# Seven block products instead of eight in six groups of layer one's second mixing product

## The chip, the core and the metric

The kernel runs on one core of a Trainium2 chip. The core has a matrix engine, TensorE (PE in the profile; PEld is its weight load), a vector engine, VectorE (DVE), a scalar engine, ScalarE (ACT), GpSimd (POOL), and SyncE (SP), from whose queue nearly all transfers are issued. The metric is device time in microseconds (us), the median over several executions.

## The reference

Two layers run over x of 2048 tokens by 1024 features in bf16. Each is an attention part and a mixing part, both with the residual added:

```python
x = x + _A_ref(_layernorm(x), A_wqkv, A_wo)
x = x + _B_ref(_layernorm(x), B_w1, B_b1, B_w2, B_b2)
# _A_ref: qkv = x @ wqkv; 32 heads of 32; each token looks at 8 tokens, 2 apart, up to itself;
#         softmax; the values, times wo
# _B_ref: h = _layernorm(x); u = gelu(h^T @ w1 + b1)     # over tokens: w1 is 2048 x 3584
#         y = u @ w2 + b2                                # w2 is 3584 x 2048; y, transposed, is added to x
```

Both layers use the same weights. The mixing part works along the tokens: its first product turns 2048 tokens into 3584 hidden units for each of 1024 features, the second turns them back.

## The kernel before

Tokens are kept in 16 tiles of 128: eight groups i, each with the even (c = 0) and the odd tokens (c = 1) of 256 neighbours. The hidden units are kept in 14 tiles `g[fb]` of 2 x 128 units by 1024 features.

**The first mixing product** (`gemm1`, L666) walks 14 blocks of 256 hidden units. Block 0 is a plain product. Blocks 1 to 13 are each computed as a 2 x 2 block product with seven block products of eight matmuls (L719) instead of eight, after sums and differences of blocks on both sides (the Strassen scheme, in the variant of Winograd). The sums need fp16 operands in a bounded range, so ACT scales the weights of each block by a power of two, which DVE derives from a bound: the largest absolute value of the block, from two reductions over the tiles (`top`), a trip through DRAM to all partitions (`share`) and a few small operations (`power`). In layer one the weight sums are computed and stored in DRAM (`keep_sums`); layer two loads them. In layer two it also scales the finished hidden tiles (`scale_g`, on DVE) and POOL forms differences of them (`hidden_sums`).

**The second mixing product of layer one** is plain (`gemm2`, L1013). For each group i, SP fetches its 256 columns of `w2` in four parts of 448 KB (`load_w2`). For each parity c, PE runs two chains of 28 matmuls of 128x128 by 512 (L1021), with every second column of the weights as its stationary operand. DVE adds the bias and the residual tile xs (L1023) and takes the statistics for the next layer's norm (L203, L205); ACT computes the root (L197, L198); DVE normalises (L211); SP stores the tile and transposes it into hT, layer two's input (L1028). Meanwhile DVE searches the `w2` tiles for their largest values (L1011, four parts per group), with which layer two scales `w2`: at the start of layer two all eight groups' bounds are shared in one trip (`share_w2`, L652) and turned into powers (`power_w2`, L659).

**The second mixing product of layer two** (`gemm2s`) already computes every group with seven block products of 14 matmuls (L908), in pairs of groups. Its moves and scalings are on ACT (L880), the weight sums on DVE. The order of the seven in one group: the first goes to a bank pa; a scaled copy of it is moved to a bank pb, where another accumulates on it; that sum is moved to a bank pc; and so on, so that the seven results are combined inside the accumulation banks, with a few moves by ACT between.

**What sets the order.** PE's instructions are issued in the order of `in_order` calls, those of another engine in the order of `chain_` calls, where each instruction is issued after the one before it on its engine. SP has one queue, in order. An entry that waits, such as a transpose waiting for its normalised tile, holds back everything behind it.

**Places.** Weight tiles turn over in a pool of nine (`wp`), residual tiles and temporaries in one of six (`x2`), values and small unit tiles in one of 16 (`vh`), the hidden tiles in one of 14 (`gop`), scaled weight pairs in one of two (`qp`), broadcasts in another of two (`pcp`). `Pm`, `kT` and `qB` belong to the attention and are free during the mixing part.

## Time and profile before

The time is 1223.34 us, the median of three runs (1223.07 to 1223.37). The profiled execution took 1223.0 us, and its span, from the first instruction to the last, is 1221.3 us. TensorE's granted clock is 1.00 throughout.

| stage, us of the span | length | PE busy | DVE | ACT | POOL | DMA share |
|---|---|---|---|---|---|---|
| start and value projection, layer one, 0 to 65 | 65.0 | 63.4 | 38.8 | 30.0 | 2.4 | 0.83 |
| attention, layer one, 65 to 203 | 138.0 | 134.9 | 110.2 | 95.1 | 0.0 | 0.28 |
| output projection, 203 to 262 | 59.0 | 58.6 | 50.1 | 27.4 | 23.6 | 0.59 |
| first mixing product, plain block, 262 to 274 | 12.0 | 11.9 | 9.4 | 10.4 | 12.0 | 0.64 |
| first mixing product, 13 blocks, 274 to 431.4 | 157.4 | 156.7 | 106.1 | 107.0 | 0.9 | 0.60 |
| second mixing product, 431.4 to 624.8 | 193.4 | 192.5 | 114.3 | 9.5 | 0.0 | 0.49 |
| value projection, layer two, 624.8 to 680 | 55.2 | 54.9 | 9.3 | 18.4 | 0.0 | 0.07 |
| attention, layer two, 680 to 820 | 140.0 | 136.8 | 96.0 | 95.7 | 0.0 | 0.20 |
| output projection and plain block, 820 to 891 | 71.0 | 70.5 | 52.9 | 34.3 | 35.8 | 0.65 |
| first mixing product, 13 blocks, 891 to 1048 | 157.0 | 156.3 | 31.2 | 64.8 | 28.1 | 0.53 |
| second mixing product, 1048 to 1221 | 173.0 | 169.2 | 111.3 | 58.6 | 5.8 | 0.37 |

The DMA share is the mean busy share of the core's 16 DMA engines. In the lines of the profile that follow, L12 is line 12 of the kernel; `out<-in` are tiles by the program's names; a group's line ends in its busy time, the mean of one instruction in ns, and the idle time ahead of its instructions with what ended it. A line of the timeline has start, length, engine, line, operation, tiles, shape and count; brackets give a wait and its releaser. A line of a stretch (A:B) has its length and then busy time and count of PE, PEld, DVE, ACT and POOL, the granted clock, the DMA share and GB/s. A line of the DMA list has the tiles, queue, kind, count, KB of each, and the median time from issue to landing.

### The profile page before, as it was taken

The page shows a single profiled execution, that of the slowest core. Times are in us where ns is not written, and L with a number is a line of the kernel's source. Part 1 is how long each engine was busy: PE and PEld are TensorE (multiplying, and loading weights), DVE is VectorE, ACT ScalarE, POOL GpSimd, SP SyncE. Part 2 cuts the span into 40 slices and gives each one's busy share as a digit, 9 for nine tenths or more (in the row PEclk, how much of TensorE's full clock was granted, in tenths as well). Part 3 has the DMA queues.
Part 4 walks back from the last instruction along what each step waited for, and adds up shares of the span by engine and source line. Part 5 has one row for each costly group of instructions (what it writes and reads, how often), then busy time and mean ns, then how long its engine had stood idle before and what let it go on. Part 6 is the DMA issues. An engine that isn't in the chain of part 4 may idle for free.

```text
span 1221.3 us, 20012 instructions
## 1 busy us (share of the span) xinstructions
PE 1205.6 (99%) x7946; PEld 559.8 (46%) x8088; DVE 729.6 (60%) x1298; ACT 551.2 (45%) x924; POOL 108.7 (9%) x107
## 2 busy tenths in 40 slices
PE   9999999999999999999999999999999999999998
PEld 4444444444444444444444444444444444444444
DVE  7558887888777346565650467778711212785664
ACT  5457775467666610000013577764543444432342
POOL 0000000290000000000000000002722112200000
PEclk9999999999999999999999999999999999999999
DMA  8922233566565635545520110234946564264520
GB/s 235 153 62 72 82 105 104 165 199 200 167 201 163 203 89 147 135 133 148 162 78 1 44 46 20 77 110 139 309 130 197 155 190 135 72 189 129 154 80 35
DMA packets 217837, 159.28 MB, mean 130 GB/s; under 512 B 46864, under 2 KB 193936, under 8 KB 214416
## 3 DMA queue, kind: packets, MB, share of 16 engines
q1 hardware_dynamic: 217744, 158.01, 44.7%
q8 instruction: 63, 1.03, 0.4%
q14 instruction: 30, 0.25, 0.1%
HBM read 115.49 MB, written 30.43 MB: 119 GB/s over the span
## 4 chain that ended last, share of the span: by engine, by line
PE 98%; issue 1%; DVE 0%; DMA 0%; ACT 0%; DVEq 0%
PE m L399 18%; PE s L719 12%; PE m L515 9%; PE s L1021 8%; PE m L719 8%; PE s L908 7%; PE a L719 6%; PE m L384 5%; PE m L1021 4%; PE a L1021 4%; PE m L908 4%; PE s L288 3%; PE a L908 3%; PE s L595 2%; PE s L430 2%; PE a L288 1%
## 5 line engine op out<-in xcount | busy, mean ns | idle before, releaser
L399 PE MATMUL m<-hT,wqk 128*128 128x512 bf16 x963 | 223.5, 379 | 6.3 <-issue 4.6
L446 DVE TENSOR_TENSOR Pm<-pc,band 32x640 bf16<-32x640 bf16 x256 | 123.6, 483 | 53.9 <-ACT pc L434 47.1
L399 PEld LDWEIGHTS <-wqk 128*128 128x128 bf16 x1024 | 95.3, 98 | 117.9 <-issue 10.7
L1021 PEld LDWEIGHTS <-w 128*128 128x128 bf16 x896 | 87.7, 98 | 105.7
L719 PEld LDWEIGHTS <-Sw 128*128 128x128 f16 x832 | 81.4, 98 | 98.1
L197 ACT ACTIVATE ln<-mv,eps 128x1 f32<-128x1 f32 x64 | 18.9, 295 | 230.4 <-DVE mv L205 185.1
L515 PE MATMUL m<-wo,oT 128*128 128x512 bf16 x500 | 110.8, 379 | 0.9 <-issue 0.3
L1021 PE MATMUL s<-g,w 128*128 128x512 bf16 x439 | 97.5, 379 | 0.5
L719 PEld LDWEIGHTS <-w 128*128 128x128 f16 (+1 forms) x624 | 61.1, 98 | 73.6
L609 POOL TENSOR_TENSOR T<-h 128x512 f16<-128x512 bf16 x16 | 18.4, 1152 | 809.9 <-DMA xr<-xb 560.9
L410 DVE COPY qB<-qs 32x512 bf16<-32x512 bf16 x136 | 38.2, 281 | 72.1 <-ACT qs L406 70.0
L515 PEld LDWEIGHTS <-oT 128*128 128x128 bf16 x512 | 49.6, 98 | 60.6 <-issue 1.9
L719 PE MATMUL s<-T,Sw 128*128 128x512 f16 x288 | 66.1, 379 | 0.0
L434 ACT ACTIVATE pc<-s,shift 128x320 bf16<-128x320 f32 x128 | 60.8, 531 | 11.2 <-PE s L430 11.2
L609 DVE TENSOR_TENSOR py<-pz,m 128x512 f32<-128x512 f32 x14 | 9.6, 688 | 92.5 <-PE m L719 66.2
L1011 DVE TENSOR_REDUCE mx<-w 128x1 f32<-128x1792 bf16 x32 | 63.0, 2010 | 0.0
L406 ACT CAST qs<-m 128x512 bf16<-128x512 f32 x64 | 37.5, 585 | 44.3 <-PE m L399 41.9
L403 ACT CAST kT<-m 128x512 bf16<-128x512 f32 x64 | 37.5, 585 | 41.9 <-PE m L399 38.8
L384 PE MATMUL m<-wv,hT 128*128 128x512 bf16 x251 | 55.2, 379 | 0.3
L522 DVE TENSOR_TENSOR xn<-m,xr 128x512 bf16<-128x512 f32 x64 | 44.1, 689 | 15.2 <-PE m L515 14.6
L719 PE MATMUL m<-T,Sw 128*128 128x512 f16 x224 | 52.9, 379 | 0.0
L719 PE MATMUL a<-h,w 128*128 128x512 bf16 x224 | 52.9, 379 | 0.0
(172 smaller groups left out, 1817.0 us busy)
## 6 DMA issues: line engine op xcount, KB each, us to landing
w<-in_B_w_dram SPq DMA_DIRECT2D x86, 512.0 KB, 5.6
w<-in_B_w_dram SPq DMA_DIRECT2D x32, 448.0 KB, 3.7
sd<-Sw SPq DMA_DIRECT2D x13, 1024.0 KB, 6.3
Sw<-sd SPq DMA_DIRECT2D x13, 1024.0 KB, 4.9
wqk<-in_A_wqkv_dram SPq DMA_DIRECT2D x16, 512.0 KB, 5.0
xa<-xn SPq DMA_DIRECT2D x32, 256.0 KB, 2.2
xs<-xa SPq DMA_DIRECT2D x32, 256.0 KB, 3.0
wo<-in_A_wo_dram SPq DMA_DIRECT2D x8, 512.0 KB, 5.4
```

What stands on the lines that cost most here:

```text
L288: r = nc.tensor.matmul(pss_[k][n][:], lhsT=hT[:, kt, cols(*order[k])], rhs=wv[kt // 2][:, kt % 2, n * 512:(n + 1) * 512], start=(kt == 0), ...
L384: nc.tensor.matmul(ps[:], lhsT=hT[:, kt, cols(c, i)], rhs=wv[kt // 2][:, kt % 2, n * 512:(n + 1) * 512], start=(kt == 0), stop=(kt == KD - 1))
L399: mm = nc.tensor.matmul(ps[:], lhsT=wts[part][:, kt, (g % 2) * P:(g % 2 + 1) * P], rhs=hT[:, kt, lo:lo + 512], start=(kt == 0), stop=(kt = ...
L410: nc.vector.tensor_copy(out=qB[u % 2][hp, h, ls], in_=qs[hp, :])
L434: nc.scalar.activation(out=pc[:, 2 * n:2 * n + 2].rearrange("p t h k -> p (t h k)"), in_=ss[n][:, 0:2 * HG * GW], func=ACT.Exp, scale=scal ...
L446: mm = nc.vector.tensor_tensor(out=Pm[rp, :, s0:s0 + HB, r * KG:r * KG + GW].rearrange("p h t k -> p t h k"), in0=pc[rp], in1=mk, op=ALU.mult)
L515: mm = nc.tensor.matmul(ps[:], lhsT=oT[g][:, cols(c, i)], rhs=wo[n][g // 4][:, g % 4, :], start=(g == 0), stop=(g == NG - 1))
L522: return nc.vector.tensor_tensor(out=xn[:, xs_], in0=pss_["o", n][:], in1=xr[:, xs_], op=ALU.add)
L719: r = nc.tensor.matmul(out, lhsT=lhs[:, k, :], rhs=rhs[k], start=start and k == 0, stop=stop and k == NI - 1, skip_group_check=True)
L908: r = nc.tensor.matmul(out, lhsT=lhs[k], rhs=rhs[k][:, cols_], start=start and k == 0, stop=k == K - 1, skip_group_check=True)
L1011: return nc.vector.tensor_reduce(out=mx2[:, i, n:n + 1], in_=w2t[n][:], op=ALU.max, axis=AX.XY, apply_absolute_value=True)
L1021: nc.tensor.matmul(ap, lhsT=w2t[ft // HF][:, ft % HF, c::DIL], rhs=g[ft // GF][:, ft % GF, lo:lo + w], start=(ft == 0), stop=(ft == FT - 1))
```

## The change

In layer one's second mixing product, groups 0 and 1 stay plain, in four chains of 28 matmuls each. Groups 2 to 7 are computed as 2 x 2 block products, with seven block products of 14 matmuls in place of eight. The blocks are: units of even and odd tiles on one side, the two halves of the features (`lo`, `hi`) and the two parities on the others. That needs the scaled hidden tiles (`scale_g`), which layer one did not have; differences of hidden tiles (T1 to T4: `NT3` on POOL during group 0; T2 on DVE at its end, T1 in group 1, T4 in groups 1 and 2); and for each group the powers of two of its weights before its sums are formed.

The bounds of these groups' weights therefore have to be known earlier. Each `w2` group is fetched once more in seven pieces of 256 KB, into spare places (`room`: `Pm`, then parts of hT not yet written), from the third block of the first mixing product on; ACT takes a bound of a piece with one pass of absolute values and a sum over each partition (`bound_act`); a few are taken by DVE (`bound_dve`). `share_w2` and `power_w2` now work on two groups at a time and stand at places written out by hand: for groups 2 and 3, 4 and 5, 6 and 7 in this stage, for 0 and 1 in layer two's first mixing product, after 28 reductions in layer two's attention (`top_load`, `top2`).

Within a group i from 2 on, ACT also scales the four quarters of the weights of group j = i + 1 (`scaled`: A22 = q[j][:, 0], S1 = q[j][:, 1], U2, U4, four instructions each), DVE forms their sums (`mix`), and `corner` and `quarter` bring the results back to scale with bias and residual. The order of every queue in the stage, SP's included, is now written out. The 32 searches on DVE, `gemm2` and the one `share_w2` at layer two's start go.

```diff
...
+    def share_w2(i0, nb=NB2):
+        i1 = i0 + 2
+        chain_("DVE", lambda: nc.vector.tensor_reduce(out=mx3[:, i0:i1], in_=mx2[:, i0:i1, 0:nb], op=ALU.max, axis=AX.X))
+        bcw[i0] = pcp.tile([P, P, 2], FP32, name="bcw", tag="pc")
+        nc.sync.dma_start(out=mxw[i0 // 2][:], in_=mx3[:, i0:i1])
+        return nc.sync.dma_start(out=bcw[i0][:], in_=mxw[i0 // 2][:].partition_broadcast(P))
+
+    bcw = {}
+
...
+        chain_("DVE", powers, i0, i1, bcw.pop(i0)[:].rearrange("p q i -> p i q"), cs2, ci2)
...
+        chain_("DVE", ts, inv2[:, i0:i1], ci2[:, i0:i1], gi[:])
+        chain_("DVE", ts, ncs2[:, i0:i1], cs2[:, i0:i1], -1.0)
+        chain_("DVE", ts, k[:], cs2[:, i0:i1], gs[:])
...
+        chain_("DVE", tt, nc.vector, bia[:, i0:i1, 1], bia[:, i0:i1, 1], k[:], ALU.mult)
...
+    room = [Pf[:, n * 1024:(n + 1) * 1024].rearrange("p (f s) -> p f s", s=256) for n in range(NPM)]
...
+    def fetch(dst):
+        i, n = jobs.pop(0)
+        fetched.append((i, n, dst))
+        return nc.sync.dma_start(out=dst,
+                                 in_=w2_v[:, 4 * n:4 * n + 4, i * 256:(i + 1) * 256])
...
+    def bound_act(i, n, src):
+        return nc.scalar.activation(out=src, in_=src, func=ACT.Abs, accum_out=mx2[:, i, n:n + 1])
...
+    def bounds(eng, n):
+        for _ in range(n):
+            i, k, src = fetched.pop(0)
+            chain_(eng, bound_act if eng == "ACT" else bound_dve, i, k, src)
...
+        def late_work(fb):
+            n = fb - (NFB - 3)
+            for f in range(*((0, 4), (4, 9), (9, 13))[n]):
+                chain_(V, scale_g, f)
...
+            if first and fb > 1:
+                for _ in range(2 if fb < 5 else 1):
+                    with tc.issue_after(kept.ins):
+                        fetch(room.pop(0))
+            if first and fb >= 4:
+                bounds(A, 1)
...
+            if first and fb == NFB - 3:
+                hidden_scale()
...
+            if first and fb >= NFB - 3:
+                late_work(fb)
...
+            if not first and fb == 2:
+                share_w2(0, 2 * NB2)
+            if not first and fb == 5:
+                power_w2(0)
         if first:
-            chain_(V, hidden_scale)
...
+    def gemm2f(g, src, dst, seam):
...
+        def scaled(i, out, f, c, ns=range(4)):
+            for n in ns:
+                chain_(A, lambda: nc.scalar.activation(out=part(out, n), in_=raw(i, f, c, n), func=ACT.Identity,
+                                                       scale=cs2[:, i:i + 1]))
...
+        def mix(out, x, y, op):
+            for o, a_, b_ in zip(pieces(out), pieces(x), pieces(y)):
+                chain_(V, tt, nc.vector, o, a_, b_, op)
...
+        def load_x(i):
+            for c in range(DIL):
+                xs[i, c] = x2("xs")
+                chain_("SP", nc.sync.dma_start, out=xs[i, c][:], in_=rows(src, c, i))
...
+        def load_w(i):
...
+                chain_("SP", nc.sync.dma_start, out=w[i][n][:], in_=w2_v[:, f0:f1, i * 256:(i + 1) * 256])
...
+        def corner(i, c, h, src_):
+            tq = x2("tq", [P, 512], FP32)
+            chain_(A, move, tq[:], src_, scale=gi[:], bias=b2_sb[:, i, c:c + 1])
...
+        def corner_add(i, c, h):
+            x = xs[i, c][:, halves[h]]
+            chain_(V, tt, nc.vector, x, tqs.pop((i, c, h))[:], x, ALU.add)
+            stat_half(i, c, h)
...
+        def quarter(i, c, h, src_):
+            x = xs[i, c][:, halves[h]]
+            chain_(V, lambda: nc.vector.scalar_tensor_tensor(out=x, in0=src_, scalar=inv2[:, i:i + 1], in1=x, op0=ALU.mult,
+                                                             op1=ALU.add))
...
+        def aggregate(i, c):
+            chain_("SP", nc.sync.dma_start, out=rows(dst, c, i), in_=xs[i, c][:])
+            mvs[i, c] = st("mv", [P, 2])
+            chain_(V, lambda: nc.vector.bn_aggr(out=mvs[i, c][:], in_=t[i, c][:]))
+
+        def root(i, c):
+            ln, rss[i, c] = st("ln", [P, 1]), st("rs", [P, 1])
+            chain_(A, lambda: nc.scalar.activation(out=ln[:], in_=mvs[i, c][:, 1:2], func=ACT.Ln, bias=eps1[:], scale=1.0))
+            chain_(A, lambda: nc.scalar.activation(out=rss[i, c][:], in_=ln[:], func=ACT.Exp, scale=-0.5))
...
+        def normalise(i, c):
+            xn = kT[1]
+            chain_(V, norm_dve, xn[:], xs[i, c][:], mvs[i, c][:, 0:1], rss[i, c][:])
+            chain_("SP", nc.sync.dma_start_transpose, out=hT[:, :, cols(c, i)], in_=xn[:])
+
+        def refill(n):
+            for _ in range(n):
+                chain_("SP", fetch, room.pop(0))
...
+        load_w(0)
+        load_x(0)
+        room[:] = [hT[:, m:m + 4, (c * NI + i) * P:(c * NI + i + 2) * P] for i in (6, 4) for c in range(DIL) for m in (0, 4)]
+        refill(8)
+        load_w(1)
+        chain_(A, ln_exp_table)
+        grp = [(0, 1), (1, 1), (0, 0), (1, 0)]
...
             for ft in range(FT):
-                nc.tensor.matmul(ap, lhsT=w2t[ft // HF][:, ft % HF, c::DIL], rhs=g[ft // GF][:, ft % GF, lo:lo + w],
-                                 start=(ft == 0), stop=(ft == FT - 1))
-            nc.vector.scalar_tensor_tensor(out=xo[:, lo:lo + w], in0=ap, scalar=b2_sb[:, i, c:c + 1],
-                                           in1=xs[:, lo:lo + w], op0=ALU.add, op1=ALU.add)
-        nc.sync.dma_start(out=dst, in_=xo[:])
-        mean, rs = stats(xo, 1.0, eps1)
-        last["DVE"] = norm_dve(xs[:], xo[:], mean, rs[:])
-        nc.sync.dma_start_transpose(out=hT[:, :, cols(c, i)], in_=xs[:])
-        for n in range(2 * c, 2 * c + 2):
...
+        bk = [[t_[:] for t_ in two("s") + two("s")], [t_[:] for t_ in two("a") + two("m")]]
+        in_order(tokens, 0, 0)
+        bounds(A, 4)
+        corner(0, 0, 1, bk[0][0])
+        corner_add(0, 0, 1)
+        share(2)
+        in_order(tokens, 0, 1)
+        bounds(A, 4)
+        for k in range(K):
+            chain_(G, tt, nc.gpsimd, T3(k), B22[k], B12[k], ALU.subtract)
+        corner(0, 1, 1, bk[0][1])
+        corner_add(0, 1, 1)
...
+        in_order(tokens, 0, 2)
+        bounds(A, 3)
+        del room[:5]
+        corner(0, 0, 0, bk[0][2])
+        corner_add(0, 0, 0)
...
+        root(0, 0)
+        normalise(0, 0)
+        in_order(tokens, 0, 3)
+        load_w(2)
+        load_x(1)
+        bounds(A, 1)
+        refill(5)
+        units_a(2)
+        units_b(2)
+        units_c(2)
+        corner(0, 1, 0, bk[0][3])
+        corner_add(0, 1, 0)
+        aggregate(0, 1)
+        scaled(2, q[2][:, 0], 1, 1)
+        root(0, 1)
+        t2(*range(4))
+        normalise(0, 1)
+        t2(*range(4, K))
+        in_order(tokens, 1, 0)
+        corner(1, 0, 1, bk[1][0])
+        scaled(2, q[2][:, 1], 0, 1)
+        scaled(2, U2[2], 0, 0)
+        corner_add(1, 0, 1)
+        mix(q[2][:, 1], q[2][:, 1], q[2][:, 0], ALU.add)
+        bounds(A, 5)
+        in_order(tokens, 1, 1)
+        corner(1, 1, 1, bk[1][1])
+        scaled(2, U4[2], 1, 0)
+        mix(U2[2], q[2][:, 1], U2[2], ALU.subtract)
+        for k in range(K):
+            chain_(V, tt, nc.vector, T1[k], B12[k], B11[k], ALU.subtract)
+        corner_add(1, 1, 1)
+        share(4)
+        refill(4)
+        bounds(A, 1)
+        in_order(tokens, 1, 2)
+        corner(1, 0, 0, bk[1][2])
+        corner_add(1, 0, 0)
+        aggregate(1, 0)
+        t4(*range(4))
+        bounds(A, 2)
+        root(1, 0)
+        normalise(1, 0)
+        power_w2(4)
+        t4(*range(4, 8))
+        bounds(A, 1)
+        in_order(tokens, 1, 3)
+
+        for i in range(2, NI):
+            j = i + 1
+            more = j < NI
+            pa, pd, pb, pc = (t_[:] for t_ in (two("a") + two("m") if i % 2 else two("s") + two("s")))
+            A22, S1, S2, S4 = q[i][:, 0], q[i][:, 1], U2[i], U4[i]
+            load_x(i)
+            if more:
+                load_w(j)
+                refill({2: 8, 3: 2}.get(i, 0))
+            else:
+                seam()
+            in_order(product, pa, stripes(i, 0, 0), B11)
+            if i == 2:
+                corner(1, 1, 0, bk[1][3])
+                corner_add(1, 1, 0)
+            else:
+                quarter(i - 1, 1, 0, prev)
+            aggregate(i - 1, 1)
+            chain_(A, move, pb, pa, scale=cs2[:, i:i + 1], bias=bia[:, i, 0:1])
+            root(i - 1, 1)
+            mix(S4, S4, S2, ALU.subtract)
+            normalise(i - 1, 1)
+            if i in (3, 4):
+                bounds(V, min(1, len(fetched)))
+            in_order(product, pd, weights(S1), T1)
+            if more:
+                units_a(j)
+                scaled(j, q[j][:, 0], 1, 1)
+            Z = x2("z", [P, 512], FP32)
+            chain_(A, move, Z[:], pd)
+            if more:
+                scaled(j, q[j][:, 1], 0, 1)
+            in_order(product, pb, weights(S2), [T2k(k) for k in range(K)], False)
+            mix(S1, A22, S2, ALU.subtract)
+            S3 = S1
+            if i == 2:
+                t4(*range(8, K))
+            if i == 3:
+                bounds(V, 1)
+            chain_(A, move, pc, pb, bias=bia[:, i, 1:2])
+            if i == 4:
+                bounds(A, len(fetched))
+                share(6)
+            if more:
+                units_b(j)
+                scaled(j, U2[j], 0, 0, range(2))
+                mix(q[j][:, 1], q[j][:, 1], q[j][:, 0], ALU.add)
+            in_order(product, pa, stripes(i, 1, 0), B21, False)
+            corner(i, 0, 0, pa)
+            corner_add(i, 0, 0)
+            if more:
+                scaled(j, U2[j], 0, 0, range(2, 4))
+            bounds(A, {2: 3, 3: 2}.get(i, 0))
+            in_order(product, pc, weights(S3), NT3, False)
+            Y = x2("y", [P, 512], FP32)
+            chain_(V, tt, nc.vector, Y[:], Z[:], pc, ALU.add)
+            quarter(i, 1, 1, Y[:])
+            if more:
+                mix(U2[j], q[j][:, 1], U2[j], ALU.subtract)
+            in_order(product, pb, weights(S4), B22, False)
+            chain_(V, tt, nc.vector, Z[:], Z[:], pb, ALU.add)
+            quarter(i, 0, 1, Z[:])
+            if more:
+                units_c(j)
+                scaled(j, U4[j], 1, 0)
+            aggregate(i, 0)
+            root(i, 0)
+            normalise(i, 0)
+            if i == 4:
+                power_w2(6)
+            in_order(product, pc, weights(A22), [T4k(k) for k in range(K)], False)
+            prev = pc
+        i = NI - 1
+        quarter(i, 1, 0, prev)
+        aggregate(i, 1)
+        root(i, 1)
+        normalise(i, 1)
...
+            if vis % 4 == 0 and vis < 4 * (DIL * NPRE if first else NB2):
+                chain_("SP", pre_load if first else top_load, vis // 4)
...
-            if first and 0 <= k < DIL * NPRE:
+            if 0 <= k < (DIL * NPRE if first else NB2):
                 with tc.issue_after(divided.ins):
-                    pre_top(k, j)
...
+        hT = new_hT()
...
+        def seam():
+            wv[:] = load_wv()
+            fill_wv(wv)
+            chain_("SP", load_qk, 0, wts)
+
+        gemm2f(g, xa[li], xb, seam)
+        qB = new_qB()
+        chain_("DVE", zero_fill)
...
```

## The prediction

> **What bounds the kernel now.** I read the busy shares, then the chain that ended last, then the stage's own lines. TensorE (PE) is busy 99% of the span and carries 98% of the chain; the other engines have room.

> ```profile
> PE 1205.6 (99%) x7946; PEld 559.8 (46%) x8088; DVE 729.6 (60%) x1298; ACT 551.2 (45%) x924; POOL 108.7 (9%) x107
> PE 98%; issue 1%; DVE 0%; DMA 0%; ACT 0%; DVEq 0%
> ```

> The stage that is rewritten runs from 431.40 to 624.79 us. The timeline below, inside it, gives the rate (56 products from 443.49 to 455.57: 0.2157 us each) and the chain behind a finished tile: PE ends, VectorE (DVE) adds, statistics, ScalarE (ACT) root, normalise, and 3.1 us after PE's end SP issues the transpose.

> ```profile
> 443.49 12.25 PE L1021 MATMUL a<-g,w 128*128 128x512 bf16 x55
> 443.69 0.75 DVE L1023 SCALAR_TENSOR_TENSOR xo<-s,b_sb,xs 128x512 bf16<-128x512 f32 x1 [4.56 <-PE s L1021]
> 444.48 0.69 DVE L203 BATCH_NORM_STATS2 bn<-xo 128x6 f32<-128x512 bf16 x1
> 445.20 0.21 DVE L205 BATCH_NORM_AGGREGATE mv<-bn 128x2 f32<-128x12 f32 x1
> 446.01 0.55 DVE L211 TENSOR_SCALAR xs<-xo,mv,rs 128x1024 bf16<-128x1024 bf16 x1 [0.60 <-ACT rs L198]
> 446.62 1.28 SPq L1028 DMA_TRANSPOSE hT<-xs  x1
> 447.99 0.53 SPq L1015 DMA_DIRECT2D xs<-xa  x1
> ```

> Transfers matter next. The first stretch holds that transpose alone and ends with its bytes (from finer stretches: 447.8 to 449.4); the second is layer two's second mixing product, fetching `w2` alone: 298 GB/s with the DMA engines full. The issue list gives landing times.

> ```profile
> 447.50:449.50 2.00, 2.00 (x11) 0.88 (x9) 2.00 (x2) 0.00 (x0) 0.00 (x0) 1.00 0.93 148
> 1109.00:1120.00 11.00, 11.00 (x53) 4.97 (x51) 3.37 (x6) 2.41 (x4) 0.00 (x0) 1.00 1.15 298
> ```

> ```profile
> w<-in_B_w_dram SPq DMA_DIRECT2D x32, 448.0 KB, 3.7
> xs<-xa SPq DMA_DIRECT2D x32, 256.0 KB, 3.0
> mxw<-mx SPq DMA_DIRECT2D x1, 4.0 KB, 1.4
> ```

> Rows that price the new work, and (last) nine products at the start of the span, in 4.02 us, 0.43 us apart or so where 0.2157 is usual:

> ```profile
> L880 ACT ACTIVATE qa<-w,cs 128x512 f16<-128x512 bf16 x24 | 15.5, 709 | 0.0
> L555 ACT ACTIVATE h<-xn,bi,rs 128x1024 bf16<-128x1024 bf16 x32 | 39.7, 1240 | 23.1 <-DVE bi L541 23.1
> 1091.43 4.57 ACT L880 ACTIVATE qa<-w,cs 128x512 f16<-128x512 bf16 x8
> 1057.35 4.77 DVE L609 TENSOR_TENSOR U<-g 128x512 f16<-128x512 bf16 x14
> 1.05 4.02 PE L309 MATMUL s<-warm 128*128 128x512 bf16 x9 [1.05 <-DVE warm L113]
> ```

> **Removed.** A group had 112 products (24.16 us). Groups 2 to 7 get 7 x 14 = 98 (21.14 us): 84 fewer, 84 x 0.2157 = 18.1 us, all on the path. DVE's 32 searches (63 us), the one `share_w2` and its powers lay beside PE: nothing.

> **Added before the stage: nothing on the path.** In layer one's first mixing product a block lasts 12.08 us; ACT is busy 106.6 of 157 us there (busy time by stretches), 8.2 a block. One bound (128x1024, the 1.24 row, some 1.15 back to back) fits into that; it overruns ACT's 1.1 us gap ahead of the first GELU by little, and 1.7 us of idle before a later GELU takes that up. Without this cover: at most ten times 0.3 us. 15 fetches of 256 KB (0.9 us each at 298 GB/s) enter SP's queue behind `keep_sums`, where DMA is 60% busy. 13 `scale_g` (0.75 each) fall in three blocks that no longer have two `top` reductions (2.28 each); the 14th ends 2 us after the stage begins, and PE reads that block 5.6 us in.

> **Added after it: nothing.** Layer two's attention gets 28 reductions of 0.675 us, 18.9 on DVE (96 of 140 us busy), and 14 loads on SP; layer one's attention carries 24 of the same with DVE at 110 of 138 us, and PE is as busy there. `power_w2(0)` is a dozen small DVE operations in a stage where DVE is busy 31 of 157 us. Zeroing Pm and qB (2.8 + 2 x 1.8 us) has 55 us of value projection over it.

> **Inside a group: ACT's queue order costs.** Per group ACT has 16 scalings (eight took 4.57 us, so about 9.3), three moves, one corner and two roots, some 13 of 21.1 us; DVE some 13 too. Load alone does not bind. But the move into bank pc, which the fifth product waits for, stands behind eight scalings of group i+1, and the first four wait for that group's `w2` loads. On SP those stand behind the transpose of (i-1, 0), which ends group i-1. So there is a loop, longer than the group:
> - transpose issue to last `w2` part landed: transpose bytes done after 2.8 us; two xs (0.5 MB) and four w (1.835 MB) at 298 GB/s, 7.85; landing 0.9 (3.7 less a 1.2 start and 1.5 of bytes): 11.6.
> - ACT: last part 0.5, Z move 0.5, four scalings 2.3, pc move 0.65, hand-over 0.15: 4.1.
> - PE: products five and six, 6.04.
> - DVE ends a mix (0.35), Z add 0.68, quarter 0.75, statistics 0.9, roots and normalise 1.3: 4.0.

> That is 25.7 us against 21.14: PE waits 4.6 us before product five in groups 3 to 6, 18.4 in all. At the window's fastest slices (350 GB/s) it is 3.4 a group; with a slower landing (the longest of the `w2` loads in layer two's stage took 8.4 us, the median 5.5) 6. Group 7 prepares nothing and waits for nothing.

> [...]

> **Into group 2** (us from the stage's start). `share(2)` goes out at 9.2 behind 3.9 MB of loads, its broadcast lands about 18; `power_w2(2)` holds DVE to 20.3, so the transpose of (0,0) leaves at 22.9 and `w2` of group 2 lands at 32.9. ACT then runs root, corner, eight scalings, five bounds, a corner and four scalings to 47.9. DVE, through the T1 series at 46.1, issues `share(4)` at 47.6; the next fetch stands behind both of its DMAs (1.5 us for the write) and lands at 52.5. ACT waits for it, then has four bounds, two corners and a root before the move into pb: 59.6. PE wanted it at 48.3 + 6.04 = 54.4: 5.3 us. The transpose of (1,0) leaves at 57.8, `w2` of group 3 lands 11.6 later, pc is ready at 73.3 against 65.7: 7.7 more. Sum 13.0. A bound is priced between 1.0 (half the 128x2048 row of 1996 ns) and 2.0; with nine in the chain, and `share(2)`'s write landing in 1.4 rather than some 6 us, 8 to 18.

> **PE after a wait.** Nine products back to back would take 9 x 0.2157 + 0.2 = 2.1 us (55 of them end 0.4 after 55 x 0.2157); the row has 4.02, though the granted clock's column says 1.00: 1.9 lost on starting from idle. The longest wait of PE's queue elsewhere is 0.4 us, and nothing is lost after it. The five waits of group 2's product five and of groups 3 to 6 (4.6 to 7.7 us) lie between: 0 to 1.9 each; I take half, 4.8. A slow stretch after group 2's first wait would be hidden, as its second wait ends by DMA and ACT.

> **Sum:** the profiled execution took 1223.0 us (span 1221.3; the median of the runs, 1223.34, is 0.3 above). 1223.0 - 18.1 + 18.4 + 13.0 + 4.8 = 1241.1.

> **Rivals.**
> - *Loads hidden.* PE runs through all groups: 1223.0 - 18.1 = 1204.9. For it: 13 of 21.1 us on both engines. It needs the last `w2` part within 7.0 us of the transpose's issue, not 11.6. With group 2's waits alone: 1218. Chance 0.11, 1211 or so between.
> - *Waits, no slow restart.* 1236.3, since short gaps cost nothing in this trace. 0.30.
> - *Every wait restarts slowly.* 5 x 1.9: 1245.8; more where a slow stretch outlasts nine products. 0.22. [...]
> - *Bounds dear.* At 2.0 us nine bounds delay group 2 by 7 more, first block still hidden: 1248. 0.05; in the range.

> My forecast has 0.32.

> **How the numbers follow.** The forecast is 1241.1, the likeliest single case. The low end, 1226: 3.4 a group (13.6), 8 in group 2, no slow restart, on 1204.9 (1226.5). The high end, 1256: 6 x 4 + 18 + 9.5 on 1204.9 (1256.4). The hidden case lies outside. A measurement tells about 0.2% (2.4 us) from no change. Faster 0.11 (hidden, or half hidden), same 0.03, slower 0.86.

> **What would show it.** PE with waits of 4 to 6 us ahead of product five in groups 3 to 6, on ACT's move into pc; ACT waiting there on a DMA of w; two waits in group 2; none in groups 0, 1, 7; the first mixing product and layer two's attention as long as before. Products of 0.43 us after a wait decide between the middle cases. I am wrong if SP issues the `w2` loads well before the group begins, or they land within 7 us.

## The result, and the profile after

The changed kernel is slower: 1258.62 us (1255.04 to 1260.57) against 1223.20 us, a ratio of 1.0286 with an interval of 1.0263 to 1.0310. The forecast was 1241.1, its range 1226 to 1256. The profiled execution took 1258.13 us with a span of 1256.4. The page's busy shares and its chain, which read 99% and "PE 98%" before:

```profile
PE 1211.3 (96%) x8004; PEld 554.6 (44%) x8004; DVE 754.3 (60%) x1454; ACT 669.5 (53%) x1130; POOL 125.2 (10%) x121
PE 92%; DMA 4%; ACT 2%; DVE 1%; SPq 0%; issue 0%; DVEq 0%
```

TensorE (PE) is still the bound, but 8% of the chain is now others'. The list of waits for PE, from 426 to 670 us (line, what it waited for, total, times, longest), comes to 40.1 us; before, the list is empty. The chain's 8% is more than that, because the chain follows the other engines' work back to before the wait began:

```profile
PE s L1120 <- ACT s L1125: 17.5, 2, 12.7
PE s L1120 <- DVE qa L610: 12.5, 2, 7.1
PE m L1120 <- DVE qa L610: 10.1, 2, 5.7
```

PE's timeline places the six waits (start, length, then the chain; the wait is in brackets):

```profile
498.71 4.60 PE L1120 MATMUL s<-T,u 128*128 128x512 f16 x14 [12.72 <-ACT s L1125]
503.15 3.19 PE L1120 MATMUL s<-g,w 128*128 128x512 bf16 x14
513.45 5.28 PE L1120 MATMUL s<-Pm,qa 128*128 128x512 f16 x12 [7.12 <-DVE qa L610]
541.67 4.44 PE L1120 MATMUL m<-Pm,qa 128*128 128x512 f16 x12 [4.35 <-DVE qa L610]
569.49 4.44 PE L1120 MATMUL s<-Pm,qa 128*128 128x512 f16 x12 [4.82 <-ACT s L1125]
598.21 5.28 PE L1120 MATMUL m<-Pm,qa 128*128 128x512 f16 x12 [5.72 <-DVE qa L610]
627.78 4.48 PE L1120 MATMUL s<-Pm,qa 128*128 128x512 f16 x12 [5.41 <-DVE qa L610]
```

The first stands at product 3 of group 2, the others at product 5 of groups 2 to 6 (`Pm` holds NT3, product 5's right side). Group 7 has none. Where DVE is named as the releaser, ACT's move into pc ended within 0.06 us of DVE's instruction (541.62 and 541.67 in group 3). An undisturbed product takes 3.02 us from start to start, as groups without waits show; those behind the waits took 4.44, 5.58, 4.71, 4.70, 5.87 and 4.75.

The stage's account: from its first product to layer two's first value projection it took 193.39 us before and takes 228.28 now, 34.9 more. The 84 products saved are -18.1; the waits are 40.1; the slow products 11.9; six times 0.17 us is the part of a chain's modelled end that overlaps the next start and is therefore missing from each wait, 1.0. The sum is 34.9. The rest of the kernel is as long as before within 0.2 us.

Group 3 shows the loop. ACT's timeline:

```profile
533.33 0.72 ACT L1099 ACTIVATE qa<-w,cs 128x512 f16<-128x512 bf16 x1 [3.83 <-DMA w<-in_B_w_dram]
537.86 0.51 ACT L1099 ACTIVATE qa<-w,cs 128x256 f16<-128x256 bf16 x1 [0.19 <-DMA w<-in_B_w_dram]
538.27 0.58 ACT L1125 ACTIVATE z<-a 128x512 f32<-128x512 f32 x1
538.75 2.33 ACT L1099 ACTIVATE qa<-w,cs 128x512 f16<-128x512 bf16 x4
540.98 0.64 ACT L1125 ACTIVATE m<-m,bia 128x512 f32<-128x512 f32 x1
```

and SP's queue in the same stretch:

```profile
526.02 1.24 SPq L226 DMA_TRANSPOSE hT<-kT  x1
527.36 1.00 SPq L226 DMA_DIRECT2D xs<-xa  x2
528.46 4.62 SPq L226 DMA_DIRECT2D w<-in_B_w_dram  x4
```

The transpose of (2, 0) leaves at 526.02, the four parts of group 4's `w2` go behind it, the last is there at 537.86, and the move that PE waits for (`m<-m,bia`) stands behind the scalings that need them.

Ahead of group 2's first wait there is another chain, in the timelines of ACT, then DVE, then SP:

```profile
480.21 2.34 ACT L1099 ACTIVATE u<-w,cs 128x512 f16<-128x512 bf16 x4
492.00 1.06 ACT L691 ACTIVATE hT<-hT 128x1024 bf16<-128x1024 bf16 x1 [9.46 <-DMA hT<-in_B_w_dram]
497.92 0.74 ACT L1125 ACTIVATE s<-s,bia,cs 128x512 f32<-128x512 f32 x1
```

```profile
482.63 0.15 DVE L657 TENSOR_REDUCE mx<-mx 128x2 f32<-128x14 f32 x1
```

```profile
482.81 0.34 SPq L659 DMA_DIRECT2D mxw<-mx  x1
487.09 0.32 SPq L660 DMA_DIRECT2D bcw<-mxw  x1
487.50 2.04 SPq L687 DMA_DIRECT2D hT<-in_B_w_dram  x4
```

ACT stands 9.46 us for a fetch. That fetch waits in SP's queue until the write of `share(4)` has landed and its broadcast has left, and the write leaves only when DVE is through T1.

### The profile page after: what moved, and what is told of

Read it like the earlier page. It is cut to its first block, busy times and chain, and to the rows that moved or that the text cites. A ratio compares the mean times of both kernels' runs of the same rounds, so it can differ in the third digit from the quotient of the medians.

```text
span 1256.4 us, 20473 instructions
## 1 busy us (share of the span) xinstructions
PE 1211.3 (96%) x8004; PEld 554.6 (44%) x8004; DVE 754.3 (60%) x1454; ACT 669.5 (53%) x1130; POOL 125.2 (10%) x121
## 4 chain that ended last, share of the span: by engine, by line
PE 92%; DMA 4%; ACT 2%; DVE 1%; SPq 0%; issue 0%; DVEq 0%
PE m L400 18%; PE s L770 12%; PE m L516 9%; PE m L770 8%; PE s L970 7%; PE a L770 6%; PE m L385 4%; PE s L1120 4%; PE m L970 4%; PE s L289 3%; PE a L970 3%; PE m L1120 3%; DMA w<-in_B_w_dram 3%; PE s L596 2%; PE s L431 2%; PE s L1213 2%
## 5 line engine op out<-in xcount | busy, mean ns | idle before, releaser
L400 PE MATMUL m<-hT,wqk 128*128 128x512 bf16 x1024 | 231.8, 380 | 0.0
L610 POOL TENSOR_TENSOR T<-h 128x512 f16<-128x512 bf16 x16 | 18.4, 1152 | 666.7 <-DMA xr<-xb 417.6
L516 PEld LDWEIGHTS <-oT 128*128 128x128 bf16 x512 | 49.6, 98 | 60.6 <-issue 1.9
L610 POOL TENSOR_TENSOR Pm<-g 128x512 f16<-128x512 bf16 x24 | 28.1, 1190 | 280.9 <-ACT Pm L691 162.1
L1120 PEld LDWEIGHTS <-qa 128*128 128x128 f16 x252 | 27.0, 108 | 65.7 <-issue 34.3
L610 DVE TENSOR_TENSOR xs<-tq,xs 128x512 bf16<-128x512 f32 (+1 forms) x30 | 21.5, 718 | 52.7 <-ACT tq L1125 35.5
L556 ACT ACTIVATE h<-xn,bi,rs 128x1024 bf16<-128x1024 bf16 x32 | 39.7, 1241 | 23.1 <-DVE bi L542 23.1
## 6 DMA issues: line engine op xcount, KB each, us to landing
xa<-xn SPq DMA_DIRECT2D x32, 256.0 KB, 2.2
xs<-xa SPq DMA_DIRECT2D x32, 256.0 KB, 3.4
hT<-in_B_w_dram SPq DMA_DIRECT2D x27, 256.0 KB, 5.5
```

What stands on the lines that cost most here:

```text
L400: mm = nc.tensor.matmul(ps[:], lhsT=wts[part][:, kt, (g % 2) * P:(g % 2 + 1) * P], rhs=hT[:, kt, lo:lo + 512], start=(kt == 0), stop=(kt = ...
L516: mm = nc.tensor.matmul(ps[:], lhsT=oT[g][:, cols(c, i)], rhs=wo[n][g // 4][:, g % 4, :], start=(g == 0), stop=(g == NG - 1))
L556: normed[:] = [nc.scalar.activation(out=h2[c][i][:], in_=xn[:], func=ACT.Identity, bias=t["bi"][:], scale=t["rs"][:])]
L610: return eng.tensor_tensor(out=out, in0=a, in1=b, op=op)
L1120: r = nc.tensor.matmul(out, lhsT=lhs[k], rhs=rhs[k], start=start and k == 0, stop=k == K - 1, skip_group_check=True)
```

## The experiments

Times of whole kernels mix two things here: the rewritten stage, and waits ahead of it that come in some executions only (third part below). So for each run two lengths are given beside the time: where the stage begins (431.4 us before, 431.44 in the first profile after), and its length (193.39 and 228.28; with all 84 products saved and no wait it would be 175.3).

### Take the loop apart

**Loads earlier.** The slots of the next `w2` tiles are free as soon as product 4 of the group two before has read them, so the loads can leave there.

```diff
             if more:
-                load_w(j)
+                if i == 2:
+                    load_w(j)
                 refill({2: 8, 3: 2}.get(i, 0))
...
             in_order(product, pa, stripes(i, 1, 0), B21, False)
+            if j + 1 < NI:
+                load_w(j + 1)
             corner(i, 0, 0, pa)
```

> Edit: the loads of w2 for group i + 2 leave SP right behind product 4 of group i, ahead of the store and the transpose of (i, 0); group 3's loads stay where they are. Theory (a loop: the loads stand behind the transpose, ACT scales, PE needs the move behind the scalings): the four waits of groups 3 to 6 before product 5 (4.35, 4.82, 5.72 and 5.41 us, 20.3 together) go, and with them the slow products behind them (1.7 + 1.7 + 2.8 + 1.7 = 7.9 us): 1258.6 - 28.2 = 1230.4. Group 2's two waits stay as they are (12.7 and 7.1 us). Rival (ACT's and DVE's own work between two groups is what is too long, whatever the loads do): waits of 3 us or more stay in groups 3 to 6, and the time above 1245.

It took 1232.30 us (ratio 1.0077, 1.0062 to 1.0092); the stage 197.34 us, from 437.61 on. PE's list of waits in the stage is down to group 2's two:

```profile
PE s L1120 <- ACT s L1125: 12.3, 1, 12.3
PE s L1120 <- DVE qa L610: 6.5, 1, 6.5
```

The waits of groups 3 to 6 are gone entirely; PE runs from 523.15 us to the stage's end without a break. The loop is shown, and it is the place of SP's loads, not ACT's or DVE's work, that makes it.

**The move first, loads unmoved.** Two runs change queue orders only. The first puts the move into pc ahead of the scalings on ACT:

```diff
             if more:
-                units_a(j)
-                scaled(j, q[j][:, 0], 1, 1)
-            Z = x2("z", [P, 512], FP32)
-            chain_(A, move, Z[:], pd)
-            if more:
-                scaled(j, q[j][:, 1], 0, 1)
...
             chain_(A, move, pc, pb, bias=bia[:, i, 1:2])
...
+                scaled(j, q[j][:, 0], 1, 1)
+                scaled(j, q[j][:, 1], 0, 1)
                 scaled(j, U2[j], 0, 0, range(2))
```

> Edit: in ACT's queue the move into pc goes ahead of the eight scalings A22 and S1 of the next group; the loads stay. Theory (PE waits for the move only because it stands behind scalings that wait for loads): the waits before product 5 go in groups 2 to 6, 7.1 and 20.3 us, and the slow products behind them (2.6 + 7.9 us): 1258.6 - 37.9 = 1220.7; group 2's first wait of 12.7 us stays. Rival (the weights of group i + 1 are then late, scaled and summed only after PE wants them): PE waits instead at the second or third product of groups 3 to 7, as long as before, and the time stays within 5 us of 1258.6.

It took 1243.22 us (1.0169, 1.0144 to 1.0195), the stage 209.51. Neither expectation held: the waits at product 5 went, and new ones of 3.02, 1.67, 5.13, 2.04 and 3.47 us came at product 7 of groups 2 to 6, on DVE's Y. I took DVE's sum of S1, which stands ahead of Y, for the cause, and moved it behind Y's quarter in a second run:

```diff
-                mix(q[j][:, 1], q[j][:, 1], q[j][:, 0], ALU.add)
...
             quarter(i, 1, 1, Y[:])
             if more:
+                mix(q[j][:, 1], q[j][:, 1], q[j][:, 0], ALU.add)
```

> Edit: the changed kernel with its loads where they are; in ACT's queue the move into pc goes ahead of the scalings A22 and S1 (as in the earlier run), and now DVE's sum of S1 too goes behind the addition Y and its quarter, which stood behind it and held product 7 up. Theory (what PE waited for in that earlier run was Y, behind a sum that waits for scalings that wait for loads): the waits at products 5 and 7 of groups 2 to 6 go, 3.0, 1.7, 5.1, 2.0 and 3.5 us there with some 3.6 us of slow products, 1243 - 19 = 1224; group 2's first wait of 12 to 13 us stays. Rival (the weights of the next group come too late whatever the order): the waits move to product 2 or 3 of groups 3 to 7, and the time stays above 1238.

1250.03 us (1.0213, 1.0198 to 1.0229), the stage 215.49: the theory fell, since the waits stayed at product 7 (3.42, 3.56, 3.42, 5.85 and 2.16 us); the rival, with waits at product 2 or 3, did not come true either. DVE's timeline of that run, and then ACT's, name the cause:

```profile
518.35 0.69 DVE L610 TENSOR_TENSOR xs<-tq,xs 128x512 bf16<-128x512 f32 x1 [7.63 <-ACT tq L1125]
519.69 0.67 DVE L610 TENSOR_TENSOR y<-z,s 128x512 f32<-128x512 f32 x1
```

```profile
512.80 0.72 ACT L1099 ACTIVATE qa<-w,cs 128x512 f16<-128x512 bf16 x1 [1.09 <-DMA w<-in_B_w_dram]
516.34 1.32 ACT L1099 ACTIVATE u<-w,cs 128x512 f16<-128x512 bf16 x2
517.56 0.76 ACT L1125 ACTIVATE tq<-s,b_sb,gi 128x512 f32<-128x512 f32 x1
```

Now the corner (`tq`) stands behind the scalings; DVE waits for it 7.63 us in group 2, and 7.4 to 11.9 us in the next four, and comes to Y late. No run moved the corner, so this is read from the trace alone. Whatever stands behind scalings that wait for loads is late; moving one instruction out names the next.

### The slow products

```diff
+            nxt = [t_[:] for t_ in (two("s") + two("s") if i % 2 else two("a") + two("m"))] if more else None
+            if more:
+                in_order(idle_fill, nxt[0], {3: 18, 4: 18, 5: 18, 6: 18}.get(i, 0), stripes(i, 0, 0), B11)
             in_order(product, pc, weights(S3), NT3, False)
```

`idle_fill` issues so many products into the next group's first bank; nobody reads them.

> Edit: in groups 3 to 6, 18 products whose result nobody reads (128x512, into the bank that the next group's first product overwrites) stand between products 4 and 5, 18 x 0.2157 = 3.9 us of PE time each. They wait for nothing, so PE is busy in most of the time in which it waited. Theory (PE falls to half its rate after a wait of some microseconds, and needs some microseconds of work to come back): what is left of the waits, 0.5 to 1.8 us, is too short for that, the granted clock stays at 1.00 in groups 3 to 6, and product 5 takes 3.2 us there in place of 4.7 to 5.9: 1258.6 - 7.9 = 1250.7 with 72 more matmuls. Rival (product 5 is slow for its operands or for its turn of banks, not for the wait before it): product 5 is as slow as it was, and the time is 1258 or above.

It took 1254.34 us (1.0254, 1.0235 to 1.0273). The time is off the expectation because the stage begins late (436.86 us) in this run; the stage itself took 219.83 us, 8.5 less than 228.28, where 7.9 was expected. PE's timeline in group 3 shows the filler and product 5 behind it, and a stretch (length, then busy time and count of PE, PEld, DVE, ACT, POOL, the granted clock, DMA share, GB/s) its clock:

```profile
542.17 4.05 PE L1288 MATMUL s<-g,w 128*128 128x512 bf16 x18
546.83 2.75 PE L1120 MATMUL m<-Pm,qa 128*128 128x512 f16 x12 [0.61 <-DVE qa L610]
549.41 0.59 PE L1120 MATMUL m<-kT,qa 128*128 128x512 f16 x2
```

```profile
541.00:550.00 9.00, 8.39 (x40) 3.72 (x38) 2.48 (x4) 7.74 (x15) 0.00 (x0) 1.00 0.62 144
```

The 12 products that took 4.44 us in the changed kernel take 2.75, with the same operands and banks, and the granted clock stays at 1.00. More work made the stage shorter: the idle time before it is what makes product 5 slow. (Group 5 kept a wait of 2.76 us, and its product 5 ran at full rate behind it; the last section says when a wait is followed by slow products.)

### Ahead of the stage

The four runs above begin the stage at 435.3 to 437.6 us, though their code up to there is the changed kernel's. The changed kernel was run again in the next set, beside one without the fetches:

> The changed kernel itself once more, beside the next three on one chip. In its first profile PE has no wait in layer one's first mixing product; in the profiles of the four experiments before, whose code there is the same, it has one to three of 0.4 to 2.7 us at a block's third product, with slow products behind the longest, 4 to 6 us in all, as DVE stands up to 3.0 us behind a w1 bound's broadcast. Theory (there is just no margin left, so that it depends on the chip and the execution): 1255 to 1262, with or without such a wait. Rival (it came from the edits, through code or places): no wait before 431 us, and 1258.

1263.29 us (1.0317, 1.0299 to 1.0335); in its profile the stage begins at 433.11, after a PE wait of 1.58 us at 412.40. So the same kernel costs 1258.6 in one set of runs and 1263.3 in another.

```diff
-                    with tc.issue_after(kept.ins):
-                        fetch(room.pop(0))
+                    i_, n_ = jobs.pop(0)
+                    fetched.append((i_, n_, room.pop(0)))
```

> Edit: the 15 fetches of w2 in layer one's first mixing product are left out; ACT's ten bounds there stay, over what the places happen to hold, so the bounds of two groups' weights are not those of w2. Theory (the fetches, 256 KB each and one to two a block, delay the trip of each w1 bound through DRAM, write to broadcast, from 4.4 us before to 7.5 and more): the write lands within 6 us again, DVE does not wait for a broadcast, PE not for ACT, and the first mixing product's 13 blocks take 157 us: 5 us less than the changed kernel where that has the wait, and no more than 1 us less where it has none. Rival (ACT's ten bounds of 1.1 us each make the moves late): the waits stay as they are in the changed kernel on this chip.

1258.27 us (1.0281, 1.0265 to 1.0296), 5.0 less than the changed kernel beside it; the stage begins at 431.29 and is as long as before (227.55 against 227.94). Between the two profiled executions the difference is 1.8 us, the later start of the stage; where the other executions lose the rest, no profile shows. The fetches, not ACT's bounds, make the waits that the profiles show. The trip of the last w1 bound through DRAM shows how. SP's queue, the write `mxd` and the broadcast `bc`, first the kernel before, then the changed kernel in its second profile:

```profile
389.36 0.32 SPq L689 DMA_DIRECT2D mxd<-mx  x1
393.77 0.32 SPq L691 DMA_DIRECT2D bc<-mxd  x1
```

```profile
393.57 2.62 SPq L740 DMA_DIRECT2D mxd<-mx  x1
402.29 0.34 SPq L742 DMA_DIRECT2D bc<-mxd  x1
```

and DVE in the latter, where the broadcast is used:

```profile
407.74 0.42 DVE L634 TENSOR_REDUCE m<-bc 128x1 f32<-128x256 f32 x1 [2.12 <-DMA bc<-mxd]
```

Before, that reduction ran at 405.56 without a wait for a broadcast that had left at 393.77. The first profile after had the broadcast leave at 400.37 and use it at 405.81, with nothing to spare. One part of my expectation did not hold: without fetches the write still took 7.3 us to the broadcast's issue (390.42 to 397.69); but this is early enough. What else than the fetches makes it longer than the 4.4 us of before is open.

### Group 2

```diff
         share(4)
-        refill(4)
...
+        refill(4)
+        share(4)
```

> Edit: on SP, the four fetches refill(4) go ahead of the two transfers of share(4), which wait for DVE and for each other. Theory (ACT is late for group 2's move into pb because its next bound waits for a fetch that stands behind the trip through DRAM: it idled 9.5 us for it, to 492.0): the fetch leaves at 479.5 in place of 487.5, ACT comes to the move 8 us earlier, the first wait of group 2 falls from 12.7 to some 5 us, and the rest of the stage moves up by as much: 1258.6 - 8 = 1250.6. Rival (what ACT waits for next, the root of (1, 0) or the corners behind DVE's T1 series, is as late): the wait stays above 10 us, and the time within 2 us of 1258.6.

1253.20 us (1.0243, 1.0228 to 1.0259), the stage 217.95 us from 437.23 on: 10.3 less than 228.28. Group 2's two waits are now

```profile
495.48 3.18 PE L1120 MATMUL s<-T,u 128*128 128x512 f16 x14 [3.69 <-ACT s L1125]
510.40 4.54 PE L1120 MATMUL s<-Pm,qa 128*128 128x512 f16 x12 [8.72 <-DVE qa L610]
```

The first fell from 12.7 to 3.69 us, and product 3 behind it ran at full rate (3.18 us); the second rose from 7.12 to 8.72. The trip through DRAM ahead of the fetch is shown as the cause of some 9 us of that wait.

### Putting the cures together

The bounds that hold ACT up ahead of group 2's move belong to groups 6 and 7 and are wanted in group 4. With early loads for all groups they go behind the move:

```diff
-        share(4)
-        refill(4)
-        bounds(A, 1)
         in_order(tokens, 1, 2)
+        in_order(tokens, 1, 3)
+        load_w(3)
...
-        bounds(A, 2)
...
-        power_w2(4)
...
-        bounds(A, 1)
-        in_order(tokens, 1, 3)
...
-                load_w(j)
-                refill({2: 8, 3: 2}.get(i, 0))
+                if i == 2:
+                    share(4)
+                refill({2: 8, 3: 5}.get(i, 0))
...
-            bounds(A, {2: 3, 3: 2}.get(i, 0))
+            bounds(A, {2: 5, 3: 4}.get(i, 0))
+            if i == 3:
+                refill(1)
...
-            if i == 4:
-                power_w2(6)
+            if i in (2, 4):
+                power_w2(i + 2)
```

The one before, in this expectation, is the first run of the next part, which has these two cures and late fetches.

> Edit: the one before with the 15 fetches of the first mixing product left where the change puts them. Theory: 4 to 6 us longer than that kernel on this chip if the changed kernel has the wait there, 1209 to 1213; else the same within 1 us.

1215.71 us, a ratio of 0.9935 (0.9912 to 0.9957): faster than the changed kernel by 3.8%, and than the kernel before by 0.65%. The expectation missed: not 1209 to 1213, and 2.3 us less than that other run in place of 4 to 6 more. The stage takes 181.42 us. PE's waits from 431 to 640 us are

```profile
PE s L1120 <- DVE qa L610: 2.8, 1, 2.8
PE m L1120 <- DVE qa L610: 1.1, 1, 1.1
PE s L1120 <- ACT s L1125: 0.3, 1, 0.3
```

with 1.4 us of slow products; 1.48 us of wait come ahead of the stage. Run again beside the last group of runs:

> The kernel with the early loads of w2 and the bounds for groups 6 and 7 behind group 2's move, and the first mixing product as the change has it, once more beside the next three. Theory: 1212 to 1220 as before, with waits on w1's broadcast in the first mixing product in some executions.

1217.44 us (0.9952, 0.9938 to 0.9967), the stage 182.33 us from 436.08 on: as expected, and again faster than the kernel before.

### What was tried on top of it, and failed

The fetches of the first mixing product were moved in four ways. First into its last four blocks, with up to four bounds a block:

```diff
-            if first and fb > 1:
-                for _ in range(2 if fb < 5 else 1):
+            if first and fb > 9:
+                for _ in range({10: 3, 11: 3, 12: 2, 13: 4}[fb]):
...
-            if first and fb >= 4:
-                bounds(A, 1)
+            if first and fb > 10:
+                bounds(A, {11: 1, 12: 2, 13: 2}[fb])
...
             chain_(A, gelu, fb, 1, 0, pc)
+            if first and fb > 10:
+                bounds(A, {11: 1, 12: 2, 13: 2}[fb])
+            if first and fb == 13:
+                for _ in range(3):
+                    with tc.issue_after(kept.ins):
+                        fetch(room.pop(0))
...
```

> Edit: three things together. Loads of w2 early as before (group i + 2 behind product 4 of group i, group 3's behind the end of group 1's products); the four fetches and four bounds for groups 6 and 7 that stood ahead of group 2's move, and the share of groups 4 and 5, go behind it, into groups 2 and 3; the 15 fetches of the first mixing product go into its last four blocks, where no w1 bound travels any more. Theory (those three are all that the changed kernel loses): no wait above 1 us is left, and all of the 84 products saved show: 1223.0 - 18.1 = 1204.9, up to 1208 with small rests. Rival (ACT or DVE, busier now in groups 2 and 3, or in the last blocks of the first mixing product with three to four bounds each, become late themselves): new waits of several us there, 1212 or more.

1217.98 us (0.9951, 0.9936 to 0.9966): waits of 1.10 and 0.70 us there, on ACT's moves behind the bounds, and a stage of 184.30. The theory's 1204.9 to 1208 was missed; the time is the rival's, though its waits are smaller than it said.

The next two ways were tried with early loads, the later bounds of group 2 and both queue orders of above. These orders by themselves, with the fetches where the change puts them:

> Edit: early loads of w2, the bounds for groups 6 and 7 behind group 2's move, and both queue orders of the run before it; the first mixing product as the change has it. Theory: what was left in the stage without the orders (0.3, 2.8 and 1.1 us of waits and 1.6 us of slow products in groups 2 and 3) goes: 5 us less, 1211, with the first mixing product's wait on w1's broadcast of 0 to 5 us as the spread that remains. Rival (these waits come from loads that land late, and every order waits for them): the same as without the orders, 1215 to 1216.

1223.32 us (1.0001, 0.9989 to 1.0013), the stage 189.50, 7 to 8 longer than without the orders: waits of 5.34 us at product 5 of group 3 and 2.18 at product 7 of group 4. Neither expectation held, 1211 or 1215 to 1216; where these waits come from is open. With the loads early the orders only do harm. On top of them, the fetches in the last three blocks:

```diff
-            if first and fb > 1:
-                for _ in range(2 if fb < 5 else 1):
+            if first and fb > 10:
+                for _ in range({11: 6, 12: 1, 13: 3}[fb]):
...
-            if first and fb >= 4:
+            if first and fb > 10:
                 bounds(A, 1)
...
             chain_(A, gelu, fb, 1, 1, Y[:])
+            if first and fb > 11:
+                bounds(A, 2)
...
             chain_(A, gelu, fb, 1, 0, pc)
+            if first and fb == 13:
+                bounds(A, 3)
+                for _ in range(5):
+                    with tc.issue_after(kept.ins):
+                        fetch(room.pop(0))
...
```

> Edit: the run before it, with the 15 fetches of the first mixing product moved into its last three blocks, behind the last w1 bound's broadcast, and the ten bounds of ACT there put where ACT waits for DVE (ahead of the third GELU). Theory (the fetches delay the trip of the w1 bounds, ACT's bounds only hurt where they stand ahead of a move): no wait in the first mixing product, which ends as before, at 431.4 us; 3 to 5 us less than the run before it, 1206 to 1208, with a spread of executions under 2 us. Rival (ACT's bounds in the last blocks, or the crowded start of the next stage, make something late): waits of 1 to 3 us there, and no gain.

1232.70 us (1.0070, 1.0055 to 1.0085). DVE no longer waits for a broadcast, as expected, but my own edit put ACT's first bound just behind the fetches, as ACT's timeline shows, and PE lost 6.03 us to it:

```profile
410.75 1.06 ACT L691 ACTIVATE Pm<-Pm 128x1024 bf16<-128x1024 bf16 x1 [9.51 <-DMA Pm<-in_B_w_dram]
```

And in their old blocks, but behind the broadcast:

```diff
-                share(far)
+                kept = share(far)
```

> Edit: the run before the last, with the fetches left in their blocks, but each issued behind the w1 bound's broadcast of its block in place of ahead of its write. Theory (what hurts is the fetch in SP's queue and on the DMA engines between the weights' loads and the bound's write): the write lands within 6 us as without fetches, no wait on a broadcast, and the time within 2 us of the run with the late fetches. Rival (256 KB more per block in the same engines delay the trip wherever they stand, through the loads that follow): the wait on the broadcast stays, and the time within 2 us of the run with the fetches where the change puts them.

1232.21 us (1.0065, 1.0046 to 1.0084): issued behind the broadcast, the fetches are worse than ahead of it. DVE waits 17.5 us in all for six broadcasts, and the stage begins at 444.90. The theory's mechanism fell; that its time was met (within 2 us of 1232.70) is chance. The rival's mechanism held, the wait stays, but not its time, which is 8.9 us above the 1223.32 of the fetches where the change puts them.

The last form has the fetches in the last three blocks and the first bound a block later. It was run with the two cures (the run before it, in the expectation, is the second run of them, 1217.44 us), alone, and with the two cures and one root moved:

```diff
-            if first and fb > 1:
-                for _ in range(2 if fb < 5 else 1):
+            if first and fb in (11, 13):
+                for _ in range({11: 7, 13: 3}[fb]):
...
-            if first and fb >= 4:
+            if first and fb > 11:
                 bounds(A, 1)
...
+            if first and fb > 11:
+                bounds(A, 2)
...
+            if first and fb == 13:
+                bounds(A, 4)
+                for _ in range(5):
+                    with tc.issue_after(kept.ins):
+                        fetch(room.pop(0))
...
```

and, for the last of the three,

```diff
-            root(i - 1, 1)
             mix(S4, S4, S2, ALU.subtract)
-            normalise(i - 1, 1)
...
                 scaled(j, q[j][:, 0], 1, 1)
+            root(i - 1, 1)
+            normalise(i - 1, 1)
...
```

> Edit: the run before it, with the 15 fetches of the first mixing product in its last three blocks (seven in the eleventh block, behind the last w1 broadcast, the rest in the last block), ACT's ten bounds of them from the twelfth block on, so that the first bound comes a block after its fetch. Theory (the fetches make the w1 bounds late, nothing else): no wait in the first mixing product, it ends at 431.3 to 431.5 us; waits of 4 us in groups 2 and 3 stay: 1223.0 - 18.1 + 4.3 + 1.6 = 1210.8, with a spread under 2 us. Rival (ACT's bounds, three to seven a block now, make moves or share(2) late): waits of 1 us and more there or in groups 0 to 2, and no gain on the run before it.

> Edit: the changed kernel with this move of the fetches and bounds alone. Theory: the first mixing product ends at 431.4 us without a wait; 1256 to 1259 with less spread, as where the fetches were left out (1258.3), 4 us or so under the changed kernel on the same chip (1263.3). Rival: 1262 or more.

> Edit: f1 with the root of (i - 1, 1), for which ACT waits 2.9 us on DVE's statistics at the start of a group, behind the four scalings A22 of the next group. Theory (in groups 2 and 3 the move into pc is late by that wait of ACT, since the weights are there by now): the waits of 2.8 and 1.1 us at product 5 and the 1.6 us of slow products behind the first go: 5 us less than f1, 1205 to 1207. Rival (the transpose of (i - 1, 1) is then 2 to 3 us later and holds DVE, SP or the residual loads up): waits elsewhere, and no gain.

They took 1220.86 us (0.9976, 0.9967 to 0.9986), 1266.29 (1.0348, 1.0332 to 1.0363) and 1222.09 (0.9991, 0.9981 to 1.0000). In each the time is the rival's. The first half of the theory held: the stage begins at 431.74, 431.75 and 432.29. But it is 191.14 us long with the two cures, where it was 182.33: the fetches and bounds now fall into its first group, the transpose of (0, 0) leaves 33.1 us after the stage's start (464.87) in place of 26.9 (462.96 in the run with the two cures alone), and PE waits 1.7 us for DVE's T1 and 4.4 us for the move into pb in group 2. Alone, the stage takes 235.84 us in place of 228.28, as group 2's first wait grows to 16.66 us. Moving the root gained nothing either (190.89 us). No free place for these 15 fetches was found.

## Why the prediction was right or wrong

**Right: the direction, the mechanism and the middle terms.** The seven-product groups save 18.1 us as costed (an undisturbed group takes 21.16 us). The steady wait was put at 4.6 us a group, before product five of groups 3 to 6, none in group 7; it measured 4.35, 4.82, 5.72 and 5.41, 20.3 in all against 18.4. Its parts are as near: transpose to last `w2` part 11.8 us in group 3 (11.6 forecast), from there to the move's end 3.8 (4.1), DVE's tail 3.8 (4.0: product 6's end at 549.57 to the transpose at 553.37). The slow products lie in the same loop and lengthen it, but on PE's side, so they add to the time rather than to the wait. The rival in which the loads are hidden was wrong, and the sentence that decided it, a transfer that must land within 7.0 us, was the right one. Group 2's second wait was put at 7.7 and measured 7.12. Layer two's part costs nothing, as said: from its value projection to the end 596.7 us, before 596.5.

**Wrong: "Into group 2", the first wait.** 5.3 us forecast, 12.7 measured; with the second wait, 19.8 in place of 13.0, beyond the 18 that I kept as the upper bound. Two trips through DRAM were priced too low. `share(2)` was to land at 18 us and the transpose behind it to leave at 22.9; the broadcast was used at 22.2 (453.65) and the transpose left at 27.0 (458.43). The bound was ready at 9.2 as forecast, but SP was issuing four loads until 443.70, and its write left 3.2 us later. `share(4)` was to go out at 47.6 with a write of 1.5 us; it went at 51.4, and the write took 4.3. I took the 1.4 us of the row `mxw<-mx` from an idle moment of the kernel before; here the four writes of that row took 5.6, 4.3, 3.9 and 7.1 us. The fetch then was in ACT's hands at 60.6 in place of 52.5: 3.8 us for the later start, 2.8 for the write, and 1.5 behind it. The swap of the two entries gave that back. The bounds themselves were priced well, 1.15 us against 1.04 in a row of five (474.35 to 479.55); the rival in which they are dear was wrong.

**Wrong: "PE after a wait", half of 1.9 us.** All six waits were followed by slow products, 11.9 us. The five that the prediction charged cost 10.5 against 4.8; the sixth, 1.4 us behind group 2's first wait, was rightly called hidden: the second wait ends by ACT's move, and was 1.6 us longer in the swap run, where product 3 was not slow. The rival "every wait restarts slowly" (1245.8) had this right with its 9.5, and the run with the filler shows it: the four slow products of groups 3 to 6 vanish with the idle time. Even the rival's 1.9 was short for two of them, 2.6 and 2.9 us. The half was a guess between two cases; for waits of over 4.3 us the runs know only one (last section). The prediction also took the column's 1.00 beside the nine slow products at the start for a reading: the trace's first clock record stands at 5.58 us, behind them, so the column says nothing there.

**Wrong in part: "Added before the stage: nothing on the path".** In the profiled execution of the result it cost nothing; in the second set of runs 5 us by the medians. I had looked at ACT for the bounds and at the DMA share for the fetches, but not at who waits for a transfer in that stage: DVE waits for w1's broadcast, with some 7 us of margin before, and the 15 fetches used it up. Why one set of runs falls on one side and the next on the other is open; nothing here tells a chip from an execution.

With the measured terms the sum closes: 1223.0 - 18.1 + 20.3 + 19.8 + 11.9 + 1.0 + 0.2 = 1258.1. Of the 17.0 us above the forecast, 6.8 are group 2's waits and 7.1 the slow products.

## What to carry to other kernels

When a stage is made shorter, compare its new length with every loop that runs once a pass through the other queues; a load that stands behind the last result of the pass is such a loop, and issuing it when its slot comes free (here half a pass earlier) was worth 31 us of 228. Price a small trip through DRAM by the traffic around it, not by its row in an idle moment (the writes took 3.9 to 7.1 us here, that row 1.4), and ask who waits for it. In these runs a wait of 4.3 us or more on PE cost the wait and the slow products behind it, and a wait of 2 to 3.7 us did so in part of the cases.
